# Second expert layer of the second batch element: seven block products over chunk pairs, first-layer weight parts kept in DRAM

## The chip, the cores and the metric

One NeuronCore of a Trainium2 chip runs the whole program. The metric is the device time of one execution in microseconds, as a median over runs. The engines are named as in the profile: PE (TensorE; PEld is its weight load), DVE (VectorE), ACT (ScalarE), POOL (GpSimd) and SP (SyncE, which issues the DMAs).

## The reference

Attention within clusters, then a squared-ReLU layer pair, then four experts that are weighted per token. Only the last part is touched by the change:

```python
def _moe2_ref(x, domain_probs, w1, w2):          # x is 1536 x 512: two batch elements of 768 tokens
    p = domain_probs / (domain_probs.sum(-1, keepdims=True) + 1e-09)
    out = np.zeros((N, D))
    for e in range(E):                           # E = 4 experts, F = 1024
        h = np.maximum(x @ w1[e], 0.0)           # first layer:  512 -> 1024
        out += p[:, e:e + 1] * (h @ w2[e])       # second layer: 1024 -> 512
    return out
```

All of it is float32. The kernel splits each float32 operand into a high and a low part and forms three PE products (high x high, high x low, low x high) for each product of the reference.

## The kernel before

The experts' part walks over 32 groups. A group n is one batch element (n // 16: the "first half" and the "second half" of the tokens, 768 each) and one chunk of 256 of an expert's 1024 hidden columns (16 chunks, `FQ` = 256, `NFQ` = 16).

*First layer of a group* (`product`, `block_product`, L895 to L902). Tokens (2 x 384), hidden columns (2 x 128) and the 512 inputs (2 x 256) are cut into two blocks each, and seven block products in the manner of Strassen and Winograd stand for eight. They are numbered 1, 5, 6, 2, 7, 3, 4. Each is 6 matmuls that stream 384 columns: 42 a group. Products 1, 6, 7 and 4 accumulate in one PSUM bank ("A"), 5 and 3 in another ("C"), 2 in a third ("B"). Because 6, 7 and 4 add to what is in bank A, each must wait until ACT or DVE has read the sum before it. The readings go to `fa` (`c_copy` on ACT, `c_add` on DVE), then `h_hi` (ACT: ReLU and rounding) and `h_lo` (DVE: the rest) write the parts of the hidden block into `ga` or `gb`.

*Weights of the first layer* (`fq_load`, `fq_prep`). Each group loads its 512 KB of w1 from DRAM and prepares it anew, in the second half too: the high parts on ACT, the low parts and the four sums of blocks on POOL, into the buffers `W["X"]` and `W["Y"]` (each high and low, two sides that alternate by group).

*Second layer of a group* (`token_tile`, `tile_products`, L1056 to L1097). It is a plain product: for each of the 6 tiles of 128 tokens, 6 matmuls that stream 512 columns, then one DVE instruction that multiplies by the expert's weight and adds to the output (`x2_t`). Its w2 rows are split by `second_hi` (ACT) and `second_lo` (POOL).

*Order.* It is written by hand: `group(n)` first finishes products 4 and 3 of group n - 1, runs products 1, 5, 6, 2, 7 of its own, and then the six token tiles of group n - 1, with the preparation of group n + 1 placed between them. Every engine takes its instructions in this program order. SP issues all DMAs in order; the DMAs carry eight semaphores in turn, so that one waits for the landing of the eighth before it.

Of the kernel before, what the change touches and what calls it, by code (L numbers as in the profile page):

```python
# [8 lines left out]
F32 = mybir.dt.float32  # L9
# [3 lines left out]
ALU = mybir.AluOpType  # L13
# [21 lines left out]
def moe_attention_kernel(  # L35
# [178 lines left out]
    with tc.manual_schedule():  # L214
# [755 lines left out]
        def r_lo(b, i, eng):  # L970
            eng.tensor_tensor(
                r_op(i, 1, b), t_src(b, i), r_op(i, 0, b).bitcast(F32), op=ALU.subtract)

        def fq_load(n, part=2):

            if n >= 2 * NFQ:
# [14 lines left out]

        def fq_prep(n):

            if n >= 2 * NFQ:
# [656 lines left out]

        def group(n):
            prep = fq_prep(n + 1)
            m = n - (NFQ - 6)
            if n > 1:
                fourth(n - 1)
            product(n, 1)
            c_copy(n, 0)
            if n > 1:
                third(n - 1)  # L1660
            last_relu(n - 1)
            if n == 1:
# [34 lines left out]
        NN = 2 * NFQ  # L1697
        for n in range(NN):
# [3 lines left out]
            if n:  # L1702
                group(n)
            else:
                first_group()
        fourth(NN - 1)
        third(NN - 1)
        last_relu(NN - 1)
        for t in range(NTT - 1):
            token_tile(NN - 1, t)  # L1710
        last_tile()
        mctx.close()


# [28 lines left out]
```

## Time and profile before

| | us |
|---|---|
| three timed runs: median (lowest, highest) | 1007.45 (1006.6, 1008.22) |
| the profiled execution's own time | 1007.97 |
| its span, first to last instruction | 1006.0 |
| PE busy | 998.3 |
| DVE, ACT, POOL busy | 734.4, 560.2, 607.8 |

The experts' part begins near 494 us and runs to the end. "Busy" sums the instructions of an engine; matmuls overlap, so the pace of PE is read from the chain of waits, where each piece stands with the time that it adds, and not from the mean duration of a matmul. The granted TensorE clock is 0.999 of full speed (2.4 GHz) over the whole span.

### The profile page before, as it was taken

Reading aid. Unit: us, or ns where it says so; the run is one execution under the profiler, and the core shown is the slowest. Engines: PE = TensorE matmul, PEld = TensorE weight load, DVE = VectorE, ACT = ScalarE, POOL = GpSimd, SP = SyncE. Lnnn points to the kernel's source line nnn. Section 1 sums busy time; section 2 is a strip of 40 time slices with the busy share of each in tenths; the row PEclk is TensorE's granted clock in tenths of the full one; section 3 lists DMA queues with packets and bytes.
Section 4 is the critical chain, followed back from the end, with each engine's and each line's share of the span. In section 5 each row is a group of like instructions: output and inputs, shape, how many; then the busy total and the mean of one; then the engine's idle time right before and its main releaser. Section 6 shows DMA issues by size and latency. Waiting matters only on the chain.

```text
span 1006.0 us, 15008 instructions
## 1 busy us (share of the span) xinstructions
PE 998.3 (99%) x5469; PEld 893.7 (89%) x5469; DVE 734.4 (73%) x1126; ACT 560.2 (56%) x1131; POOL 607.8 (60%) x618
## 2 busy tenths in 40 slices
PE   8999999999999999999999999999999999999998
PEld 8999999999888888888889989899899898998997
DVE  6898999888899997898585555567676555555555
ACT  6888888888655654446554344344453443444431
POOL 6468777763326604347576766767678567676671
PEclk9999999999999999999999999999999999999999
DMA  7577876862112122212012212122123221221201
GB/s 186 128 157 178 205 172 165 178 140 72 42 43 84 45 82 84 85 42 83 22 43 85 61 65 84 42 85 65 62 84 119 71 84 43 84 67 60 84 22 63
DMA packets 74082, 89.65 MB, mean 89 GB/s; under 512 B 27332, under 2 KB 50264, under 8 KB 74008
## 3 DMA queue, kind: packets, MB, share of 16 engines
q1 hardware_dynamic: 74008, 88.69, 31.9%
q8 instruction: 43, 0.70, 0.3%
q14 instruction: 31, 0.25, 0.1%
HBM read 62.58 MB, written 3.19 MB: 65 GB/s over the span
## 4 chain that ended last, share of the span: by engine, by line
PE 95%; DVE 2%; POOL 1%; DMA 1%; ACT 1%; issue 0%; SPq 0%; POOLq 0%; ACTq 0%
PE bank L900 29%; PE bank L1062 26%; PE bank L931 13%; PE s L656 6%; PE t L689 6%; PE bank L878 5%; PE po L703 3%; PE po L705 3%; PE s L878 1%; PE m L478 1%; PE m L393 1%; PE po L1114 0%; DMA k<-nkh 0%; PE m L494 0%; DVE ptl L695 0%
## 5 line engine op out<-in xcount | busy, mean ns | idle before, releaser
L1093 DVE SCALAR_TENSOR_TENSOR x<-bank,pe_p,x 128x512 f32<-128x512 f32 x179 | 134.3, 751 | 67.4 <-PE bank L1062 67.2
L1006 POOL TENSOR_TENSOR wxl<-raw,wxh 128x512 fp32r<-128x512 f32 x64 | 82.5, 1310 | 139.7 <-ACT wxh L1005 139.7
L207 ACT CAST wyh<-raw 128x512 fp32r<-128x512 f32 x64 | 39.6, 621 | 152.0 <-POOL raw L200 120.4
L1062 PE MATMUL bank<-wzh,ga 128*128 128x512 f32 (+1 forms) x392 | 121.9, 386 | 0.0
L1062 PE MATMUL bank<-wzh,gb 128*128 128x512 f32 x384 | 121.2, 390 | 0.0
L1037 DVE TENSOR_TENSOR fa<-bank,fa 128x384 f32<-128x384 f32 x96 | 53.3, 556 | 85.5 <-PE bank L900 56.4
L695 DVE TENSOR_TENSOR ptl<-t,pth 128x384 fp32r<-128x384 f32 x192 | 98.1, 549 | 20.0 <-ACT pth L694 19.6
L900 PE MATMUL bank<-xa,wxh 128*128 128x384 f32 (+1 forms) x392 | 103.9, 346 | 0.0
L665 DVE TENSOR_REDUCE nb<-s 128x1 f32<-128x768 f32 x96 | 90.9, 948 | 8.4 <-PE s L656 8.0
L694 ACT CAST pth<-t 128x384 fp32r<-128x384 f32 x192 | 83.9, 486 | 9.3 <-PE t L689 8.4
L900 PE MATMUL bank<-xa,wyh 128*128 128x384 f32 (+1 forms) x344 | 88.6, 338 | 0.0
L676 ACT ACTIVATE p<-s,nb 128x768 f32<-128x768 f32 x96 | 88.0, 916 | 0.3 <-DVE nb L665 0.2
L656 PE MATMUL s<-k,q 80*128 80x384 f32 (+1 forms) x384 | 86.5, 346 | 0.2
L1062 PEld LDWEIGHTS bank<-wzh,ga 128*128 128x128 f32 x392 | 73.3, 188 | 14.5
L689 PE MATMUL t<-identf,p 128*128 128x128 f32 x576 | 85.4, 276 | 0.4 <-DVE ptl L695 0.3
L1062 PEld LDWEIGHTS bank<-wzh,gb 128*128 128x128 f32 x384 | 72.1, 188 | 14.7
L208 POOL TENSOR_TENSOR wyl<-raw,wyh 128x512 fp32r<-128x512 f32 x64 | 84.6, 1342 | 0.0
L1034 ACT COPY fa<-bank 128x384 f32<-128x384 f32 x96 | 46.1, 480 | 66.1 <-PE bank L900 66.0
L703 PE MATMUL po<-pth,vv 128*128 128x256 f32 x288 | 80.4, 309 | 0.0
L931 PE MATMUL bank<-gb,wzh 128*128 128x512 f32 x240 | 78.0, 391 | 0.2
L900 PEld LDWEIGHTS bank<-xa,wxh 128*128 128x128 f32 x392 | 72.2, 188 | 5.6
L689 PEld LDWEIGHTS t<-identf,p 128*128 128x128 f32 x576 | 67.6, 140 | 9.5 <-DVE ptl L695 6.8
(290 smaller groups left out, 2640.8 us busy)
## 6 DMA issues: line engine op xcount, KB each, us to landing
raw<-in_moe_w_dram SPq DMA_DIRECT2D x64, 512.0 KB, 3.6
raw<-in_moe_w_in_dram SPq DMA_DIRECT2D x7, 1024.0 KB, 5.2
raw<-in_moe_w_out_dram SPq DMA_DIRECT2D x6, 1024.0 KB
k<-nkh SPq DMA_DIRECT2D x28, 192.0 KB, 3.3
q<-nqh SPq DMA_DIRECT2D x28, 192.0 KB, 4.1
nv<-in_v_dram SPq DMA_DIRECT2D x16, 192.0 KB, 4.1
out_dram<-x SPq DMA_DIRECT2D x11, 256.0 KB, 2.0
k<-nkl SPq DMA_DIRECT2D x14, 192.0 KB, 3.4
```

The costliest lines, as they stand in the source:

```text
L208: return lambda: eng.tensor_tensor(lo, a[m], hi.bitcast(F32), op=ALU.subtract)
L656: nc.tensor.matmul(s[:, j, 0:HALF], stk[i, nq][:, t * 128:(t + 1) * 128], stk[i, nk][:, j * HALF:(j + 1) * HALF], start=first, stop=not first)
L665: nc.vector.tensor_reduce(out=nb, in_=s_ps[u][:, :, 0:HALF], axis=AX.XY, op=ALU.max, negate=True)
L676: nc.scalar.activation(p, s_ps.pop(u)[:, :, 0:HALF], AF.Exp, bias=nb_t.pop(u), accum_out=sums_t[hp][:, i % 2, t:t + 1])
L689: nc.tensor.transpose(tp[:, j], p_sb[u][:, half, j * 128:(j + 1) * 128], identf)
L694: return (lambda: nc.scalar.copy(dh, tp), lambda: nc.vector.tensor_tensor(dl, tp, dh.bitcast(F32), op=ALU.subtract))
L695: lambda: nc.vector.tensor_tensor(dl, tp, dh.bitcast(F32), op=ALU.subtract))
L703: nc.tensor.matmul(po_t[pr], vt[i][:, kt], pth[:, kt], start=(kt == 0), stop=False)
L900: nc.tensor.matmul(ps, w[:, ks], x(xx)[:, kt], start=(first and kt == 0 and z == 0), stop=(kt == 1 and z == 2), skip_group_check=True)
L931: nc.tensor.matmul(o, a[:, d], b, start=(ft == 0 and z == 0), stop=(ft == 1 and z == 2))
L1062: nc.tensor.matmul(o, a, w[:, f, cols], start=(f == 0 and z == 0), stop=(f == 1 and z == 2))
L1093: nc.vector.scalar_tensor_tensor(out=acc, in0=o, scalar=pc, in1=acc, op0=ALU.mult, op1=ALU.add)
```

## The change

The first half of the tokens keeps its groups. What is new:

- *Kept weights.* At the end of each group n of the first half `keep(n + 1)` writes the prepared parts of the next chunk (six DMAs, 1.8 MB) to a DRAM tile. In the second half `back(n)` reads them into the same buffers; the loads and the preparation of chunks 18 to 31 are gone (16 and 17 are prepared as before).
- *Second layer of the second half.* Two chunks of one expert make a pair m (8 pairs). Their hidden blocks (tokens 2 x 384, hidden 2 x 256) and w2 (hidden 2 x 256, outputs 2 x 256) are again multiplied by seven block products (`second_product`). Each is 3 token tiles x 6 matmuls that stream 256 columns: 126 matmuls a pair, where six tiles of two groups had 72 that stream 512. After each tile one DVE instruction of 128 x 256 adds it to the output: 21 a pair, where 12 of 128 x 512 stood.
- *Operands.* The steps S, H, L (hidden blocks of 128 x 768: sums on DVE, high parts on ACT, low parts on DVE) and t, y, z (w2 blocks of 128 x 512: sums on POOL, high parts on ACT, low parts on POOL) make the operands of the seven products. R is a ReLU on ACT. Each operand has one buffer.
- *Order.* The two layers are interleaved by a written sequence. A pass over pair m runs its seven second-layer products (m1, m5, m6, m2, m7, m3, m4), with first-layer products of later chunks between them, and the steps of the next pair hang on these events. Before the first pass, chunks 16 to 19 run their first layer with nothing but the last token tiles of the first half between (the *hand-over*); the last pass but one has only two first-layer products left, the last has none.

```diff
+        ORDER2 = (1, 5, 6, 2, 7, 3, 4)
+        kept = {n: mp["hb"].tile([128, 4096], F32, name=f"kept{n}") for n in range(2, NFQ)}
+        KEPT = [("X", 0, 2), ("Y", 0, 4), ("X", 3, 4)]
+        def keep(n):
...
+                    nc.sync.dma_start(
+                        out=kept[n][:, o + a * 256:o + b * 256],
+                        in_=W[t][x][:, p + a * 256:p + b * 256].bitcast(F32))
...
+        def h_sum(m, i, eng=nc.vector):
+            if i == 5:
+                nc.vector.scalar_tensor_tensor(
+                    out=hx(m, 1, 0), in0=hx(m, 1, 1), scalar=0.0, in1=hx(m, 1, 0), op0=ALU.max, op1=ALU.add)
...
+            elif i == 7:
+                eng.tensor_tensor(hsum(m), hx(m, 0, 0), hx(m, 1, 0), op=ALU.subtract)
...
+        def first_product(n, i):
+            m, q = divmod(n - NFQ, 2)
+            product(n, i)
...
+            if i == 1:
+                nc.scalar.copy(hx(m, 0, q)[:, 0], a)
+            elif i == 5:
+                nc.scalar.copy(hx(m, 1, q)[:, 1], c)
+            elif i == 6:
+                nc.scalar.copy(hx(m, 1, q)[:, 0], a)
+            elif i == 4:
+                nc.scalar.activation(hx(m, 0, q)[:, 1], a, AF.Relu)
+                if n != NFQ + 1:
+                    back(n + 2)
+            else:
...
+                nc.vector.tensor_tensor(o, z, o, op=ALU.add)
...
+        def second_product(m, i):
...
+            for j in range(3):
+                o = {"A": bank[5 + j][:, 0:256], "C": bank[(2, 3, 1)[j]][:, 0:256],
+                     "B": bank[(4, 0, 4)[j]][:, 256 * (j == 2):][:, 0:256]}[b]
...
+                    for z, (a, w) in enumerate(((hh, wh), (hh, wl), (hl, wh))):
+                        nc.tensor.matmul(
+                            o, a, w, start=(i in (1, 5, 2) and f == 0 and z == 0),
+                            stop=(f == 1 and z == 2), skip_group_check=True)
...
+                    nc.vector.scalar_tensor_tensor(
+                        out=acc, in0=o, scalar=pc, in1=acc, op0=ALU.mult, op1=ALU.add)
...
+        SECOND = {"m1": "H1 y1 z1 t5 t7", "4b": "S5", "m5": "L1 H5", "m6": "S6 y5 z5 t6",
+                  "m2": "H2 H6 y6 y2 z6 z2 t4", "m7": "H7", "m3": "y7 y3 z7 z3", "m4": "H4 y4 z4"}
+        NEXT = {"5a": "L5", "6a": "L6", "7a": "L2", "1b": "S3", "3a": "H3 L7", "4a": "N1",
+                "5b": "L3", "6b": "L4"}
+        SAME = {"7a": "R0", "6b": "R1", "2b": "S7g"}
+        LATE = dict(SECOND, m2=SECOND["m2"] + " L5", m3=SECOND["m3"] + " L6", m4="H4 y4 z4 L7g")
+        LAST = {"m1": "L2 S3", "m5": "H3 L3g", "m6": "L4"}
+        FIRST = {(17, 1): "y5 z5 t6", (17, 5): "R1", (17, 2): "y6 y2 z6 z2 t4 S7g", (17, 4): "S5 H1 L1",
+                 (18, 5): "H5 S6", (18, 6): "L5 y7 y3 H6 z7 z3", (18, 2): "L6", (18, 7): "H2 y4 z4 L2",
...
+        first_product(NFQ, 5)
+        for f in prep[0:2]:
+            f()
+        for i in (6, 2, 7):
+            first_product(NFQ, i)
+        for t in range(NTT):
+            token_tile(NFQ - 1, t)
+            if t == 0:
+                steps(0, "R0")
+                first_product(NFQ, 3)
+                first_product(NFQ, 4)
...
+        for m in range(NM):
...
+            seq = "m1 3p 4p m5 m6 m2 m7 m3 1a m4 5a 6a 2a 7a 1b 3a 4a 5b 6b 2b 7b".split()
```

In `seq`, a and b are the two chunks of the pair after next, and p is the second chunk of the next pair (its products 3 and 4 come a pass later).

*ACT at the hand-over.* Before, between products 1 and 6 of a group of the second half (the two COPY rows), ACT had one ReLU of the group before:

```order
L1043 ACTIVATE ga<-bank_4442 128x384 [waits PE_49]
L1034 COPY fa<-bank_4441 128x384 [waits PE_49,Activation_49]
L1043 ACTIVATE ga<-fa 128x384 [waits DVE_49]
L1034 COPY fa<-bank_4441 128x384 [waits PE_49,Activation_49]
L1015 CAST wzh<-raw 128x1024 [waits DMAHW5_49]
```

Now, around product 5 (L1818) and product 6 (L1820) of chunk 18, it has the operand steps H1 and H5 (L1800), the copies, y7 and y3 (L1767) and H6:

```order
L1822 ACTIVATE fa<-bank_4444 128x384 [waits PE_49,Activation_49]
L1800 CAST xa<-fa 128x768 [waits Activation_49]
L1818 COPY x_4452<-bank_4445 128x384 [waits DMAHW0_49,DMAHW3_49,DVE_49,PE_49]
L1800 CAST xa<-fa 128x768 [waits DVE_49]
L1820 COPY x_4452<-bank_4443 128x384 [waits PE_49]
L1767 CAST ga<-raw 128x512
L1767 CAST wzh<-raw 128x512
```

The copy of product 6 out of bank A (4443) now stands behind H5, which waits for the DVE's S5.

*POOL and DVE at the hand-over.* Before, POOL went from one chunk's preparation to the next; now, behind the last preparation (L208), it makes z1, t5 and t7, z5, t6, z6, z2, t4 and S7 (L1792):

```order
L208 TENSOR_TENSOR wyl<-raw,wyh 128x512 [waits PE_49,Activation_49]
L1770 TENSOR_TENSOR wzl<-raw,wzh 128x512 [waits DMAHW7_49,Activation_49]
L1764 TENSOR_TENSOR raw<-raw 128x2x256 [waits Pool_49] x2
L1770 TENSOR_TENSOR wzl<-raw,wzh 128x512 [waits Activation_49]
L1764 TENSOR_TENSOR raw<-raw 128x512
L1770 TENSOR_TENSOR gb<-raw,gb 128x512 [waits DVE_49,Activation_49]
L1770 TENSOR_TENSOR gb<-raw,gb 128x512 [waits Activation_49]
L1764 TENSOR_TENSOR raw<-raw 128x2x256 [waits Pool_49]
L1792 TENSOR_TENSOR raw<-fa 128x768 [waits DVE_49]
```

The DVE's row S5 (L1785), first of the steps that follow the additions of chunk 17, waits for POOL:

```order
L1827 TENSOR_TENSOR fa<-bank_4446,fa 128x384 [waits PE_49,Activation_49]
L1785 SCALAR_TENSOR_TENSOR fa<-fa 128x2x384 [waits DVE_49,Pool_49]
L1808 TENSOR_TENSOR xa<-fa,xa 128x768 [waits Activation_49]
L1794 TENSOR_TENSOR fa<-fa 128x768 [waits DVE_49]
L1808 TENSOR_TENSOR xa<-fa,xa 128x768 [waits Activation_49]
L1827 TENSOR_TENSOR x_4451<-bank_4447,x_4451 128x384 [waits DMAHW0_49,PE_49]
```

S5 overwrites a block that S7 reads, so the whole row of POOL steps now stands ahead of it.

*DVE near the end.* Before, in the last groups, the six token tiles came with two short `h_lo` between them:

```order
L1093 SCALAR_TENSOR_TENSOR x_4449<-bank_4446,pe_p,x_4449 128x512 [waits PE_49]
L1046 SCALAR_TENSOR_TENSOR ga<-fa,ga 128x384 [waits Activation_49]
L1093 SCALAR_TENSOR_TENSOR x_4449<-bank_4447,pe_p,x_4449 128x512 [waits PE_49]
L1046 SCALAR_TENSOR_TENSOR ga<-fa,ga 128x384 [waits Activation_49]
L1093 SCALAR_TENSOR_TENSOR x_4450<-bank_4448,pe_p,x_4450 128x512 [waits PE_49]
L1093 SCALAR_TENSOR_TENSOR x_4450<-bank_4446,pe_p,x_4450 128x512 [waits PE_49]
```

Now, in the last pass but one, L5 and L6 (L1808) stand around the readings of m7 and m3, ahead of those of m4 (banks 4448 to 4450) and of the next pass's m1 (the last row):

```order
L1808 TENSOR_TENSOR xa<-x_4452,xa 128x768 [waits Activation_49]
L1861 SCALAR_TENSOR_TENSOR x_4452<-bank_4448,pe_p,x_4452 128x256 [waits PE_49]
L1861 SCALAR_TENSOR_TENSOR x_4451<-bank_4449,pe_p,x_4451 128x256 [waits PE_49]
L1861 SCALAR_TENSOR_TENSOR x_4452<-bank_4450,pe_p,x_4452 128x256 [waits PE_49]
L1861 SCALAR_TENSOR_TENSOR x_4451<-bank_4445,pe_p,x_4451 128x256 [waits DVE_49,PE_49]
L1861 SCALAR_TENSOR_TENSOR x_4451<-bank_4446,pe_p,x_4451 128x256 [waits DVE_49,PE_49]
L1861 SCALAR_TENSOR_TENSOR x_4452<-bank_4444,pe_p,x_4452 128x256 [waits DVE_49,PE_49]
L1808 TENSOR_TENSOR xa<-x_4451,xa 128x768 [waits Activation_49]
L1861 SCALAR_TENSOR_TENSOR x_4452<-bank_4448,pe_p,x_4452 128x256 [waits PE_49]
L1861 SCALAR_TENSOR_TENSOR x_4451<-bank_4449,pe_p,x_4451 128x256 [waits PE_49]
L1861 SCALAR_TENSOR_TENSOR x_4452<-bank_4450,pe_p,x_4452 128x256 [waits PE_49]
L1861 SCALAR_TENSOR_TENSOR x_4451<-bank_4448,pe_p,x_4451 128x256 [waits DVE_49,PE_49]
```

The m4 of one pass and the m1 of the next use the same three banks, and here no first-layer product stands between them.

## Rows read from the trace of the kernel before

**Rows 1.** The page, part 1: busy us, share of span, instructions.

```profile
PE 998.3 (99%) x5469; PEld 893.7 (89%) x5469; DVE 734.4 (73%) x1126; ACT 560.2 (56%) x1131; POOL 607.8 (60%) x618
```

**Rows 2.** The page, part 4: the chain that ended last, by engine.

```profile
PE 95%; DVE 2%; POOL 1%; DMA 1%; ACT 1%; issue 0%; SPq 0%; POOLq 0%; ACTq 0%
```

**Rows 3.** Busy time of each engine in the second half's stretch.

```profile
core 0: us, PE busy (x) PEld busy (x) DVE busy (x) ACT busy (x) POOL busy (x), PEclk, DMA share, GB/s
766.00:991.00 225.00, 225.00 (x1129) 203.50 (x1129) 125.94 (x191) 91.37 (x172) 147.65 (x127) 1.00 0.19 61
```

**Rows 4.** The chain in order of time: start us, us added, line, count.

```profile
735.66 8.20 PE bank L1062 x36
743.86 7.30 PE bank L900 x42
...
994.07 8.86 PE bank L1062 x48
```

**Rows 5.** The same chain in the attention: matmuls of 128 x 256.

```profile
100.13 0.12 PE po L703
...
100.72 0.12 PE po L705
100.84 0.70 PE s L656 x4
```

**Rows 6.** Groups by line and shape, DVE: count | busy us, mean ns | idle before.

```profile
L1093 DVE SCALAR_TENSOR_TENSOR x<-bank,pe_p,x 128x512 f32<-128x512 f32 x179 | 134.3, 751 | 67.4 <-PE bank L1062 67.2
L1037 DVE TENSOR_TENSOR fa<-bank,fa 128x384 f32<-128x384 f32 x93 | 51.7, 557 | 85.3 <-PE bank L900 56.4 <-ACT fa L1034 28.8
L1046 DVE SCALAR_TENSOR_TENSOR gb<-fa,gb 128x384 fp32r<-128x384 f32 x45 | 35.0, 778 | 8.9 <-ACT gb L1043 8.9
L1046 DVE SCALAR_TENSOR_TENSOR ga<-bank,ga 128x384 fp32r<-128x384 f32 x16 | 8.9, 556 | 12.6 <-ACT ga L1043 12.6
L971 DVE TENSOR_TENSOR rt<-x,rt 128x768 fp32r<-128x768 f32 x3 | 2.8, 945 | 0.0
L1074 DVE SCALAR_TENSOR_TENSOR x<-bank,pe_p,x 128x256 f32<-128x256 f32 x1 | 0.5, 483 | 0.0
```

**Rows 7.** Groups by line and shape, ACT.

```profile
L1034 ACT COPY fa<-bank 128x384 f32<-128x384 f32 x91 | 43.7, 480 | 63.6 <-PE bank L900 63.6
L207 ACT CAST wyh<-raw 128x512 fp32r<-128x512 f32 x60 | 37.3, 621 | 150.1 <-POOL raw L200 119.7 <-POOL raw L202 30.4
L968 ACT CAST xa<-x 128x768 fp32r<-128x768 f32 x3 | 2.5, 825 | 0.0
```

**Rows 8.** Groups by line and shape, POOL.

```profile
L208 POOL TENSOR_TENSOR wyl<-raw,wyh 128x512 fp32r<-128x512 f32 x60 | 79.2, 1340 | 0.0
```

**Rows 9.** Timeline of POOL, then DVE, where the second half begins: start, us.

```profile
749.31 2.17 POOL L971 TENSOR_TENSOR xa<-x,xa 128x768 fp32r<-128x768 f32 x1
754.39 2.30 POOL L1006 TENSOR_TENSOR wxl<-raw,wxh 128x512 fp32r<-128x512 f32 x2 [2.90 <-ACT wxh L1005]
759.92 2.54 POOL L208 TENSOR_TENSOR wyl<-raw,wyh 128x512 fp32r<-128x512 f32 x2
...
749.70 2.61 DVE L971 TENSOR_TENSOR xa<-x,xa 128x768 fp32r<-128x768 f32 x1
752.23 1.01 DVE L1037 TENSOR_TENSOR fa<-bank,fa 128x384 f32<-128x384 f32 x2
```

**Rows 10.** Timeline of ACT there.

```profile
748.07 0.82 ACT L968 CAST xa<-x 128x768 fp32r<-128x768 f32 x1
749.18 0.48 ACT L1034 COPY fa<-bank 128x384 f32<-128x384 f32 x1 [0.29 <-PE bank L900]
753.70 0.91 ACT L1005 CAST wxh<-raw 128x512 fp32r<-128x512 f32 x2
```

**Rows 11.** DMA, 518 to 990 us: packets, MB, share of 16 engines; issues, landing us.

```profile
q1 hardware_dynamic: 24144, 32.06, 21.1%
...
raw<-in_moe_w_dram SPq DMA_DIRECT2D x57, 512.0 KB, 3.6
```

**Rows 12.** The chain's last piece.

```profile
1002.96 0.35 DVE x L1074
```

More of the change, by code (lines that the diff above doesn't have):

```diff
@@ L974, in fq_load @@
         def fq_load(n, part=2):
-            if n >= 2 * NFQ:
+            if n >= NFQ + (2 if part == 0 else 0):
                 return
@@ L1691, in group @@
                     r_lo(1, RB11, nc.vector)
+            keep(n + 1)
             fq_load(n + 3, 0)
@@ L1695, in group @@
                 t_sum(1, (RT3, RT1, RT2, None, RT4)[m])
-        NN = 2 * NFQ
-        for n in range(NN):
+        ORDER2 = (1, 5, 6, 2, 7, 3, 4)
+        kept = {n: mp["hb"].tile([128, 4096], F32, name=f"kept{n}") for n in range(2, NFQ)}
+        KEPT = [("X", 0, 2), ("Y", 0, 4), ("X", 3, 4)]
+        def keep(n):
+            if n not in kept:
+                return
+            p = (n % 2) * 1024
+            for t, a, b in KEPT:
+                for x in range(2):
+                    o = 2048 * (t == "Y") + x * 1024
+                    nc.sync.dma_start(
+                        out=kept[n][:, o + a * 256:o + b * 256],
+                        in_=W[t][x][:, p + a * 256:p + b * 256].bitcast(F32))
@@ new lines, in back @@
+        def back(n, parts=KEPT):
+            if n >= 2 * NFQ:
+                return
+            p = (n % 2) * 1024
+            for t, a, b in parts:
+                for x in range(2):
+                    o = 2048 * (t == "Y") + x * 1024
+                    nc.sync.dma_start(
+                        out=W[t][x][:, p + a * 256:p + b * 256].bitcast(F32),
+                        in_=kept[n - NFQ][:, o + a * 256:o + b * 256])
+        W_AT = {1: ("X", 0, 1), 5: ("Y", 3, 4), 6: ("Y", 0, 1), 2: ("X", 1, 2),
+                7: ("Y", 2, 3), 3: ("Y", 1, 2), 4: ("X", 3, 4)}
@@ new lines, in h_hi2, with h_lo2 @@
+        def h_hi2(m, i):
+            if i in (2, 4):
+                nc.scalar.activation(h_op(i, 0), h_val(m, i), AF.Relu)
+            else:
+                nc.scalar.copy(h_op(i, 0), h_val(m, i))
+        def h_lo2(m, i, eng=nc.vector):
+            hi = h_op(i, 0).bitcast(F32)
+            if i in (2, 4):
+                nc.vector.scalar_tensor_tensor(
+                    out=h_op(i, 1), in0=h_val(m, i), scalar=0.0, in1=hi, op0=ALU.max, op1=ALU.subtract)
+            else:
+                eng.tensor_tensor(h_op(i, 1), h_val(m, i), hi, op=ALU.subtract)
@@ new lines, in acc_half @@
+        def acc_half(t, d):
+            if t < 4:
+                return x2_t[t // 2][:, t % 2, S + 256 * d:S + 256 * d + 256]
+            return x2_t[t - 4][:, d, S + 512:2 * S]
+        BLOCK = {1: (0, 0), 5: (1, 1), 6: (0, 1), 2: (0, 0), 7: (1, 1), 3: (0, 1), 4: (1, 0)}
+        def second_product(m, i):
+            e = m // (NQ // 2)
+            last = m == NFQ // 2 - 1
+            r, d = BLOCK[i]
+            b = PROD[i][2]
+            for j in range(3):
+                o = {"A": bank[5 + j][:, 0:256], "C": bank[(2, 3, 1)[j]][:, 0:256],
+                     "B": bank[(4, 0, 4)[j]][:, 256 * (j == 2):][:, 0:256]}[b]
+                js = slice(j * 128, (j + 1) * 128)
+                for f in range(2):
+                    hh, hl = [h_op(i, z)[:, f, js] for z in range(2)]
+                    wh, wl = [y_op(i, z)[:, f] for z in range(2)]
+                    for z, (a, w) in enumerate(((hh, wh), (hh, wl), (hl, wh))):
+                        nc.tensor.matmul(
+                            o, a, w, start=(i in (1, 5, 2) and f == 0 and z == 0),
+                            stop=(f == 1 and z == 2), skip_group_check=True)
+                t = 3 * r + j
+                pc = pe_p[:, NTT + t, e:e + 1]
+                acc = acc_half(t, d)
+                if m == 0 and i in (1, 5, 6, 4):
+                    nc.vector.tensor_scalar(acc, o, pc, None, op0=ALU.mult)
+                else:
+                    nc.vector.scalar_tensor_tensor(
+                        out=acc, in0=o, scalar=pc, in1=acc, op0=ALU.mult, op1=ALU.add)
+                if last and i in (2, 7, 3, 4):
+                    nc.sync.dma_start(out=ov[1, t][:, 256 * d:256 * d + 256], in_=acc)
@@ new lines, in call, with steps @@
+        def call(f, *a):
+            return lambda: f(*a)
+        FS = {"H": h_hi2, "L": h_lo2, "S": h_sum, "R": h_relu, "y": y_hi, "z": y_lo, "t": y_sum,
+              "N": lambda m, i: load_second(m + i)}
+        def steps(m, ws):
+            for w in ws.split():
+                FS[w[0]](m, int(w[1]), *([nc.gpsimd] if w[2:] else []))
+        NM = NFQ // 2
+        SECOND = {"m1": "H1 y1 z1 t5 t7", "4b": "S5", "m5": "L1 H5", "m6": "S6 y5 z5 t6",
+                  "m2": "H2 H6 y6 y2 z6 z2 t4", "m7": "H7", "m3": "y7 y3 z7 z3", "m4": "H4 y4 z4"}
@@ L1699, in moe_attention_kernel @@
+        for n in range(2 * NFQ):
             pb[n, "A"] = bank[n % 2]
@@ L1701, in moe_attention_kernel @@
             pb[n, "B"] = bank[4] if n else bank[3]
[L1702 to L1711, printed above, removed]
+        first_group()
+        for n in range(1, NFQ):
+            group(n)
+        load_second(0)
+        fourth(NFQ - 1)
+        prep = fq_prep(NFQ + 1)
+        first_product(NFQ, 1)
@@ new lines, in moe_attention_kernel @@
+        third(NFQ - 1)
+        last_relu(NFQ - 1)
+        first_product(NFQ, 5)
[9 more added lines that the diff above has]
+                first_product(NFQ, 4)
+            elif t == 1:
+                prep[2]()
+            elif t == 3:
+                steps(0, "y1 z1 t5 t7")
@@ new lines, in moe_attention_kernel @@
+        for n, i in [(1, 1), (1, 5), (1, 6), (1, 2), (1, 7), (2, 1), (1, 3), (1, 4), (2, 5), (2, 6), (2, 2),
+                     (2, 7), (3, 1), (2, 3), (2, 4), (3, 5), (3, 6), (3, 2), (3, 7)]:
+            first_product(NFQ + n, i)
+            steps(0, FIRST.get((16 + n, i), ""))
+            ev = "%d%s" % (i, " ab"[n - 1])
+            if n > 1:
+                steps(1, SAME.get(ev, ""))
+        for m in range(NM):
+            a, b = NFQ + 2 * m + 4, NFQ + 2 * m + 5
+            seq = "m1 3p 4p m5 m6 m2 m7 m3 1a m4 5a 6a 2a 7a 1b 3a 4a 5b 6b 2b 7b".split()
+            if m + 2 >= NM:
+                seq = [x for x in seq if x[1] not in "ab" and (x[1] != "p" or m + 2 == NM)]
+            for ev in seq:
+                if ev[0] == "m":
+                    second_product(m, int(ev[1]))
+                else:
+                    first_product({"p": a - 1, "a": a, "b": b}[ev[1]], int(ev[0]))
+                ev = ev.replace("p", "b") if ev in ("3p", "4p") else ev + "_" if ev in ("3b", "4b") else ev
+                if m + 2 < NM:
+                    steps(m + 1, SECOND.get(ev, ""))
+                    steps(m + 1, NEXT.get(ev, ""))
+                    steps(m + 2, SAME.get(ev, ""))
+                elif m + 2 == NM:
+                    steps(m + 1, LATE.get(ev, ""))
+                else:
+                    steps(m, LAST.get(ev, ""))
```

79 lines of the change are left out of this document (64 added, 15 removed).

## The prediction

> **What bounds the kernel now.** I read the page's busy times first, then the chain of waits, then the second half's stretch, then groups by shape. PE is busy for 998.3 of 1006.0 us [rows 1], and the chain that ended last is 95% PE [rows 2]: the time is PE's, and the other engines count only where PE waits for them. In the experts' second half PE is busy in all 225.00 us of the stretch, at full clock (1.00), while DVE has 125.94, ACT 91.37 and POOL 147.65, so DVE and POOL are at 56 and 66% [rows 3]. The chain shows PE's own pace: a group's first layer is 42 matmuls of 384 columns in 7.30 us, 0.1739 us each; its second layer is 36 of 512 columns in 8.20 us, 0.2278 us each [rows 4]. A pair of groups takes 31.0 us.
>
> The two paces differ by 0.0539 us for 128 columns, and 0.0539 x 4 = 0.2156 leaves 0.012 us of a 512-column matmul that doesn't shrink with its width. For 256 columns that line gives 0.1200 us. The attention has such matmuls, each with its own weight load: six from 100.13 to 100.84 us, 0.118 each [rows 5]. I take 0.120; 0.118 would be 2 us better over the half.
>
> **PE's work.** The first layer is the same 42 matmuls a group. The second layer before: 16 groups x 8.20 us = 131.2, and 0.7 more because the last piece, split finer, took 8.86 [rows 4]: 131.9. After: 8 pairs x 126 x 0.120 = 121.0. **Minus 10.9 us**, not the eighth of 131 (16.4) that seven products for eight suggest: 126 narrow matmuls carry the fixed part more often than 72 wide ones.
>
> *A rule beside this.* The Trainium skill ("TensorE: Matmul & The Clock Gate", section "Wait — 56ns, not 53.3ns?") gives a gap of columns / 2.4 plus 2.5 ns for one matmul. By it 72 wide ones take 15.5 us and 126 narrow ones 13.8, an estimated 14.2 us less over the half. The trace disagrees with it: 0.2278 against 0.2158 us at 512 columns. That the small fixed part holds for the new matmuls all the same is a rival below.
>
> **The other engines in a steady pass.** PE needs 84 x 0.1739 + 126 x 0.120 = 29.7 us.
> DVE: 21 readings of 0.483, 6 additions of 0.557 and 10 steps on 128 x 768 of 0.945 [rows 6] are 23.0 us; back to back an instruction holds the engine some 0.1 us less than its mean (two additions together took 1.01 [rows 9]), so about 20.
> ACT: 8 readings of 0.480, 7 casts of 0.621 and 9 or so wide ones of 0.825 or less [rows 7], about 15.5.
> POOL: 11 of 1.340 [rows 8] and one of 128 x 768, nearer 1.9: 16.6, while 8 subtractions and 4 sums a group for the weights are gone.
> All fit in 29.7, if DVE and POOL don't block each other. They do: at 749.70 a 128 x 768 subtraction of DVE took 2.61 us beside POOL's at 749.31 (2.17) [rows 9], where such steps alone take 0.945; and L1046 takes 0.778 us on two SBUF operands against 0.556 with one in PSUM [rows 6]. With a mean wait of 0.2 us a step (that difference), DVE has 22 to 25 us. Walking a pass with these durations, the nearest deadlines hold by 0.3 to 0.8 us: m7's accumulation after m6's readings, 4a after the DVE's addition of 7a, 7a after ACT's copy of 6a, 7b after the copy of 6b, which queues behind H3 and so behind DVE's S3. I take 0.8 us for the six full passes together, between 0 and 3 (0.5 each).
>
> The Trainium skill ("SBUF — State Buffer", section "Who interferes with whom") says that DVE, with two SBUF inputs, and GpSimd take a shared port pair by an exclusive lock. The 2.61 us agree.
>
> **Hand-over: four waits.** Here first-layer products of chunks 16 to 19 run with six token tiles only as cover.
> (a) The copy of product 6 of chunk 16 now queues on ACT behind the cast that began at 748.07, the copy of 5 (0.48) and the two weight casts (0.91, at 753.70 before) [rows 10]; it ends near 750.5. Product 7 would start at 749.97: **0.55 us**.
> (b) POOL's preparation of chunk 17 starts when POOL's and DVE's swap of the token blocks are done, at 752.3, and lasts what it lasted from 754.39 to 762.46 [rows 9]: 760.4. Then come z1, t5, t7, z5, t6, z6, z2, t4 (1.25 to 1.34 each) and S7 (1.9): 772.5. S5 waits for S7, H5 for S5, and the copy of (18, 6) stands behind H5 on ACT: 772.5 + 0.95 + 0.83 + 0.48 + hops = 775.1. Without waits PE would reach product (18, 7), which needs that copy, at 772.8. So (a) and (b) together are 2.3 us, set by POOL.
> (c) (18, 4) needs DVE's addition of (18, 7), which stands behind L1, S6, L5 and L6, and L6 behind H6, y3 and y7 on ACT: 0.5 us, 1.1 if z7 blocks a step.
> (d) (19, 7) needs the copy of (19, 6), behind H3 and H4 on ACT, behind S3 on DVE, which z3 and z4 can block: 0.4 to 2.4.
> Sum 3.2 to 5.8; with a late POOL up to 6.5. **I take 4.2**, nearer the lower end, since the durations in the walk are means and hold the engines a little too long.
>
> **End.** In the last pass but one DVE must also do L5 and L6 before the readings of m4, and m1 of the last pass overwrites m4's banks at once. With no blocking DVE keeps up (0); with each of five steps blocked by up to one POOL instruction of 1.34 the first reading of m4 comes 3.3 us after PE wants the bank. I take 1.2. The last reading is 0.483 instead of 0.35 us [rows 6, 12]: 0.1.
>
> **DMA.** `keep` adds 1.8 MB of writes to a group of 15.5 us, `back` 3.7 MB of reads to a pass, less 1 MB of w1. In the second stretch the engines moved 32.06 MB in 21.1% of 472 us, 322 GB/s when busy [rows 11]. First half: 2.9 MB in 15.5 us is 187 GB/s, 58%; second: 4.7 MB in 29.7 us, 160 GB/s, half. On SP's queue the loads stand behind the six `keep` DMAs, 6 us more; they are used over 10 us later. `back` is issued after a chunk's product 4, 12 us or more before the next use. Cover: those 12 us. I cost it at 0; a landing that is late would add up to 6 us once, at the hand-over.
>
> **Sum,** on the profiled execution's own 1007.97 us (1006.0 of span): - 10.9 + 4.2 + 0.8 + 1.2 + 0.1 = - 4.6, so 1003.4. The median of the three runs, 1007.45, lies 0.5 below that execution, so 1002.9 for the median; **forecast 1003 us**. Its own range, with the ends of each term (3.3 to 12.9 us of waits): 999.4 to 1009.
>
> **Rivals.**
> *The steady pass becomes DVE's (slower).* DVE's ten wide steps meet POOL's instructions in every pass. DVE has 20 us plus ten waits of w; it passes 29.7 at w = 0.96. For: w was 1.67 in the one case where both queues were full [rows 9]. Against: 0.2 on average over 45 instructions with POOL 66% busy [rows 3, 6], and POOL has 56% of a pass now, mostly not where DVE has most steps. At w = 1.2 a pass takes 32.1, 2.4 more, six times 14.4: 1017 us. It is slower than before from w = 1.04.
> *The cover holds.* The waits of the hand-over and the end don't reach PE, because POOL and ACT run ahead of my walk: 1007.45 - 10.9 + 0.1 = 996.7 us. Against: S5's wait for POOL stands in the program's order, and POOL's row of steps is long.
> *The fixed part vanishes at 256 columns.* The new matmuls would cost seven eighths of the old, 131.9 - 115.4 = 16.5 us less, with the same waits: 997 us. Against: the six matmuls of 128 x 256 [rows 5]. The skill's rule above points this way.
> *Late weights.* Kept parts or w2 blocks land after PE wants them, about 1 us a pass or 6 at the hand-over: 1009 us. Against: half of the DMA engines' time is free.
>
> **How the numbers follow.** About 0.2% (2 us) is what a measurement of this kernel can tell from no change: faster means below 1005.4, slower above 1009.5. Forecast 0.63, of which three quarters lie below 1005.4 (0.47) and the rest within (0.16), since both waits at their ends give up to 1009. DVE-bound passes 0.17: 0.15 slower, 0.02 within. Cover holds 0.12 and smaller fixed part 0.03: faster. Late weights 0.05: 0.02 within, 0.03 slower. That makes faster 0.62, same 0.20, slower 0.18. The range: 997.5 leaves out half of the cases of full cover, 1011 most of the DVE-bound ones, together under 0.2.
>
> **What would show it.** In the profile after: the chain's pieces of the new matmul line, 18 in 2.16 us (2.2 and more would say that the fixed part is larger); PE without idle time in the passes and about 30 us from m1 to m1; gaps of PE before (16, 7), (18, 7), (18, 4) and (19, 7), the second the largest and ended by ACT; on DVE S5 waiting for POOL; near the end m1 waiting for DVE's reading of m4. If PE is busy without gaps and DVE too is under 80%, the cover held. If wide DVE steps average over 1.9 us and every pass has gaps before m7 or 4a, the passes are DVE's. If PE waits for a DMA, the weights were late. I would be wrong at the root if 256-column matmuls in this stream took 0.125 us or more: 1,008 of them at that pace use up the 4.6 us.

## The result: slower by 8.4 us, and the profile after

The changed kernel takes 1016.1 us (median of 4 runs, 1014.7 to 1017.5), the kernel before 1007.7 beside it. The ratio is 1.0085, 95% interval 1.0068 to 1.0103: slower, and above the range of the prediction. The profiled execution has a span of 1014.3 us, 8.3 more than before.

Page of the changed kernel, part 1 (busy us, share of the span, instructions) and part 4 (the chain that ended last):

```profile
PE 991.1 (98%) x5889; PEld 906.0 (89%) x5889; DVE 787.6 (78%) x1209; ACT 576.2 (57%) x1139; POOL 609.6 (60%) x589
...
PE 83%; DVE 7%; POOL 4%; DMA 2%; issue 2%; ACT 1%; SPq 0%; DVEq 0%; POOLq 0%; ACTq 0%
```

PE was busy for 7.2 us less [rows 1], and its share of the chain fell from 95% [rows 2] to 83%: PE has less to do and now waits. DVE's part of the chain rose from 2% to 7%. The waits of PE in the second half, by line and by what ended them (us in total, times, longest us):

```profile
PE bank L1852 <- DVE x L1861: 10.3, 8, 2.5
PE bank L900 <- ACT x L1820: 3.4, 2, 2.0
PE bank L900 <- DVE x L1827: 0.5, 1, 0.5
PE bank L900 <- ACT fa L1820: 0.4, 1, 0.4
PE bank L1852 <- ACT fa L1822: 0.3, 1, 0.3
```

The first row is what the prediction doesn't have. Eight waits, one in each pass: the second layer's matmuls (L1852) wait for a DVE reading of the second layer (L1861). The other rows are the hand-over, and one of two short waits for ACT.

The view leaves out the hops between engines, so I also measured every stall as the time that PE falls behind its own pace (0.1739 us for a first-layer matmul, 0.120 for a second-layer one) in the rows of the timeline. Before, there is none over 0.25 us from 494 us on. After:

| where (start of the delayed matmul, us) | stall, us |
|---|---|
| hand-over: 749.56, 774.69, 778.62, 784.43 | 0.56 + 2.20 + 0.69 + 1.51 = 4.96 |
| last tile of m2, six full passes | 1.69 + 1.18 + 1.19 + 0.95 + 1.03 + 1.18 = 7.22 |
| last tile of m2, last two passes | 1.67 + 2.68 = 4.35 |
| before m5, two passes | 0.40 + 0.48 = 0.88 |
| last tile of m2 and m7 of the last pass, at a lower clock | 1.59 |
| sum | 19.0 |

With the forecast 10.9 us less work, 19.0 - 10.9 = + 8.1, against 8.3 of span (with the 10.6 that experiment 5 shows below, + 8.4). The account closes.

**The wait that was not foreseen.** First PE, then DVE, in the pass around 857 us (start us, us, operation, tiles, count, and in brackets the idle time before with what ended it):

```profile
854.96 3.76 PE L1852 MATMUL bank<-gb,xa 128*128 128x256 f32 x30
859.75 0.98 PE L1852 MATMUL bank<-gb,xa 128*128 128x256 f32 x6 [1.03 <-DVE x L1861]
...
855.23 0.48 DVE L1861 SCALAR_TENSOR_TENSOR x<-bank,pe_p,x 128x256 f32<-128x256 f32 x1 [0.52 <-PE bank L1852]
855.63 1.63 DVE L1808 TENSOR_TENSOR xa<-x,xa 128x768 fp32r<-128x768 f32 x1
857.18 1.26 DVE L1861 SCALAR_TENSOR_TENSOR x<-bank,pe_p,x 128x256 f32<-128x256 f32 x3
858.36 0.94 DVE L1794 TENSOR_TENSOR x<-x,x 128x768 f32<-128x768 f32 x1
859.22 0.86 DVE L1861 SCALAR_TENSOR_TENSOR x<-bank,pe_p,x 128x256 f32<-128x256 f32 x2
```

The 30 matmuls are m6 (18) and two tiles of m2 (12); the last 6 of m2 come 1.19 us late. `second_product` gives product 2's three tiles the banks 4, 0 and 4: the first tile lies in the lower half of bank 4, the third in its upper half. The program lets the third tile's first matmul wait until the first tile has been read. In the order of the changed program, that wait stands in the middle of m2 on PE:

```
L1852 MATMUL bank_4447<-gb,xa 128x256
L1852 MATMUL bank_4447<-gb,xa 128x256 [waits Pool_49]
...
L1852 MATMUL bank_4443<-gb,xa 128x256 x6
L1852 MATMUL bank_4447<-gb,xa 128x256 [waits DVE_49]
```

PE needs 0.72 us for the tile between. On DVE the awaited reading (the first of the two at 859.22) stands behind L1 (855.63), the three readings of m6 and S6 (858.36). So PE gets ahead of DVE and is stopped there, by 1.19 us in this pass and by 0.95 to 1.69 in the six full ones. The 1.69 of the first pass and the 1.67 of the last but one come where S6 took 2.08 and 2.06 us; in the five passes between it took 0.94.

### The profile page after: what moved, and what is told of

It reads as the page before. It is cut to its first block, busy times and chain, and to the rows that moved or that the text cites. A ratio compares the mean times of both kernels' runs of the same rounds, so it can differ in the third digit from the quotient of the medians.

```text
span 1014.3 us, 16370 instructions
## 1 busy us (share of the span) xinstructions
PE 991.1 (98%) x5889; PEld 906.0 (89%) x5889; DVE 787.6 (78%) x1209; ACT 576.2 (57%) x1139; POOL 609.6 (60%) x589
## 4 chain that ended last, share of the span: by engine, by line
PE 83%; DVE 7%; POOL 4%; DMA 2%; issue 2%; ACT 1%; SPq 0%; DVEq 0%; POOLq 0%; ACTq 0%
PE bank L900 23%; PE bank L931 12%; PE bank L1062 11%; PE bank L1852 8%; PE s L656 6%; PE t L689 6%; PE bank L878 5%; PE po L703 3%; PE po L705 3%; DVE x L1861 2%; DMA raw<-in_moe_w_dram 2%; DVE xa L1808 1%; PE s L878 1%; PE m L478 1%; PE m L393 1%
## 5 line engine op out<-in xcount | busy, mean ns | idle before, releaser
L1861 DVE SCALAR_TENSOR_TENSOR x<-bank,pe_p,x 128x256 f32<-128x256 f32 x156 | 72.8, 480 | 35.2 <-PE bank L1852 34.4
L1078 DVE SCALAR_TENSOR_TENSOR x<-bank,pe_p,x 128x512 f32<-128x512 f32 x90 | 67.6, 751 | 35.8 <-PE bank L1062 35.7
L1006 POOL TENSOR_TENSOR wxl<-raw,wxh 128x512 fp32r<-128x512 f32 (+1 forms) x36 | 47.1, 1328 | 70.1 <-ACT wxh L1005 70.1
L900 PE MATMUL bank<-rt,wyh 128*128 128x384 f32 (+1 forms) x264 | 71.4, 351 | 3.8 <-ACT x L1820 3.4
L705 PE MATMUL po<-ptl,vv 128*128 128x256 f32 x288 | 72.5, 281 | 0.0
L900 PE MATMUL bank<-xa,wxl 128*128 128x384 f32 (+1 forms) x196 | 67.7, 345 | 0.0
L207 ACT CAST wyh<-raw 128x512 fp32r<-128x512 f32 x36 | 22.3, 622 | 78.1 <-POOL raw L200 60.7
L1770 POOL TENSOR_TENSOR wzl<-raw,wzh 128x512 fp32r<-128x512 f32 x32 | 49.9, 1562 | 26.9 <-ACT wzh L1767 26.9
L656 PEld LDWEIGHTS s<-k,q 80*128 80x128 f32 (+1 forms) x384 | 63.4, 189 | 0.6 <-ACT p L676 0.2
L900 PEld LDWEIGHTS bank<-xa,wyh 128*128 128x128 f32 x344 | 62.0, 188 | 1.4
```

The costliest lines, as they stand in the source:

```text
L656: nc.tensor.matmul(s[:, j, 0:HALF], stk[i, nq][:, t * 128:(t + 1) * 128], stk[i, nk][:, j * HALF:(j + 1) * HALF], start=first, stop=not first)
L705: nc.tensor.matmul(po_t[pr], vt[i][:, kt], ptl[:, kt], start=False, stop=(kt == NTT - 1))
L900: nc.tensor.matmul(ps, w[:, ks], x(xx)[:, kt], start=(first and kt == 0 and z == 0), stop=(kt == 1 and z == 2), skip_group_check=True)
L1861: nc.vector.scalar_tensor_tensor(out=acc, in0=o, scalar=pc, in1=acc, op0=ALU.mult, op1=ALU.add)
```

## Experiments

**1. Product 2: multiply all three tiles, then read them.** No tile is then written into a bank that a reading of the same product still holds.

```
+            todo = [("p", 0), ("p", 1), ("p", 2), ("r", 0), ("r", 1), ("r", 2)]
+            if i != 2:
+                todo = [(w, j) for j in range(3) for w in "pr"]
-            for j in range(3):
+            for what, j in todo:
...
```

"p" stands for a tile's six matmuls, "r" for its reading.

> The changed kernel, but in product 2 of the second layer all three tiles' matmuls are issued before the first reading, so no tile of it is written into a bank that a DVE reading of the same product still holds. Theory, shared bank: the last tile of m2 waits in each of the eight passes (1.0 to 2.7 us, 11.6 us together) only because it lies in the upper half of bank 4, whose lower half DVE reads behind a long row of other steps. Then these eight gaps go, nothing else moves, and the time falls from 1016.1 to 1004 to 1006 us, a little faster than the kernel before. Rival, passes bound by DVE: DVE is late because it has too much to do; then the gaps come back before m7, m4 or product 4 of the first layer, 0.5 to 1.7 us a pass, and the time stays at 1011 or more. A mix is possible in the last pass alone (2.7 us of the 11.6), where DVE has two more wide steps.

Measured: 1002.9 us, ratio to the kernel before 0.995 (0.9936 to 0.9963), 13.3 us under the changed kernel and 1.1 under the expected 1004 to 1006. PE's waits in the second half:

```profile
PE bank L900 <- ACT x L1820: 2.6, 2, 2.0
PE bank L1855 <- ACT fa L1822: 0.4, 1, 0.4
PE bank L900 <- ACT fa L1820: 0.4, 1, 0.4
PE bank L1855 <- ACT x L1822: 0.4, 1, 0.4
```

No wait for a second-layer reading is left, none has come before m7 or m4, and all stalls together fell from 19.0 to 5.7 us: the 13.3 that the time fell. Of these, 11.6 are the eight waits; 1.6 the lower clock after the longest of them, which the expected time had not counted. DVE ran as many steps as before (1209 on both pages), so the eight waits came from the shared bank, not from too much work on DVE.

**2. S6 behind the readings of m2, banks left shared.**

```
...
-        "m6": "S6 y5 z5 t6",   "m2": "H2 H6 y6 y2 z6 z2 t4"
+        "m6": "y5 z5 t6",      "m2": "S6 H2 H6 y6 y2 z6 z2 t4"
```

> The changed kernel with DVE's step S6 (one 128 x 768 subtraction, 0.95 us alone, up to 1.9 beside POOL) queued behind the readings of m2 instead of ahead of them; the banks stay shared. Theory, shared bank behind a long row on DVE: the wait of m2's last tile is as long as what stands ahead of the reading, so it shrinks by the length of S6: in the six passes with S6 there from 1.0 to 1.7 us each to 0 to 0.7, 6 to 7 us together, and the time is about 1009 to 1010 us; the last two passes keep their waits. Rival, DVE-bound passes: the work of DVE is the same, so the waits only move to m7 or m4, and the time is 1014 to 1016 us.

Measured: 1008.5 us, ratio 1.0009 (1.0 to 1.0018), half a microsecond under the expected 1009 to 1010. DVE in the same pass:

```profile
855.02 2.07 DVE L1861 SCALAR_TENSOR_TENSOR x<-bank,pe_p,x 128x256 f32<-128x256 f32 x5
857.74 0.48 DVE L1861 SCALAR_TENSOR_TENSOR x<-bank,pe_p,x 128x256 f32<-128x256 f32 x1 [0.65 <-PE bank L1852]
858.14 1.43 DVE L1794 TENSOR_TENSOR x<-x,x 128x768 f32<-128x768 f32 x1
```

The reading of m2's first tile is now the fourth of the five at 855.02, ahead of S6. PE's stall in that pass is 0.32 us instead of 1.19; in the six full passes none is over that. The last pass keeps its 2.7, as expected; the last but one loses its 1.67 too, which I had not expected, although its S6 comes from the same table and was moved too. So the wait is as long as the row of DVE steps ahead of the reading.

**3. The next pass's second-layer weights loaded earlier.**

```
-        "7a": "L2", ... "4a": "N1"
+        "7a": "L2 N1"
```

> The changed kernel with the load of the next pass's second-layer weights issued after product 7 of the even chunk, ahead of the twelve transfers that bring kept parts back, instead of behind them. Theory, late weights: the two gaps before m5 (0.40 and 0.48 us) come from this load landing after ACT wants it, which holds the ReLU of product 4 back on ACT; they vanish, and the time is 1015.2 us, 0.9 less, hardly to be told from the changed kernel by its time, but to be seen as gaps in the trace. Rival, ACT's own row is too long: the gaps stay as they are. If the kept parts now land too late instead, new waits of PE on a transfer show in the first layer.

Measured: 1017.6 us (1016.5 to 1017.7), ratio 1.0095. What it was to remove is seen in the changed kernel's ACT, where the cast of the new weights waits for their transfer and the ReLU of product 4 (L1822) stands behind it; then in the same place the cast with the early load, which waits for nothing:

```profile
821.92 0.62 ACT L1767 CAST wzh<-raw 128x512 fp32r<-128x512 f32 x1 [1.78 <-DMA raw<-in_moe_w_dram]
822.45 0.49 ACT L1822 ACTIVATE fa<-bank 128x384 f32<-128x384 f32 x1
```

```profile
819.72 0.61 ACT L1767 CAST wzh<-raw 128x512 fp32r<-128x512 f32 x1
```

Both stalls before m5 are gone, as the theory had it. Yet the kernel is no faster: m2's stall is now 1.69 us in five of the six full passes (0.61 in the first). The reason is S6 (L1794). First the changed kernel, then this run, three of the passes from 800 to 980 us (min/median/max ns, first and last start), each with POOL's subtraction z5 (L1770) in the pass around 858 us; for this run S6 of that pass stands between them:

```profile
L1794 DVE TENSOR_TENSOR fa<-fa x3: 941/943/943, 827.2 to 951.4; 128x768 f32<-128x768 f32 x3
...
858.37 2.06 POOL L1770 TENSOR_TENSOR wzl<-raw,wzh 128x512 fp32r<-128x512 f32 x1
```

```profile
L1794 DVE TENSOR_TENSOR fa<-fa x3: 2073/2073/2076, 825.8 to 951.6; 128x768 f32<-128x768 f32 x3
...
857.29 2.08 DVE L1794 TENSOR_TENSOR x<-x,x 128x768 f32<-128x768 f32 x1
...
857.26 1.28 POOL L1770 TENSOR_TENSOR wzl<-raw,wzh 128x512 fp32r<-128x512 f32 x1
```

POOL works beside S6 in both kernels. In the changed kernel S6 begins 0.01 us ahead of z5 (858.36 and 858.37); S6 then takes 0.94 us and z5 2.06. With the weights in time POOL's row comes earlier and z5 begins 0.03 us ahead (857.26 and 857.29); z5 takes 1.28 us and S6 2.08. L1, which stands ahead of S6, takes 0.95 there for 1.63. The net is half a microsecond more ahead of the same reading. While the bank is shared, freeing ACT only moves the collision.

**4. Another order of side steps at the hand-over.**

```
...
-        first_product(NFQ, 5);  prep[0](); prep[1]();  first_product(NFQ, 6)
+        first_product(NFQ, 5);  first_product(NFQ, 6);  prep[0](); prep[1]()
-  (17, 5): "R1", (17, 2): "y6 y2 z6 z2 t4 S7g", (18, 2): "L6", (18, 7): "H2 y4 z4 L2",
-  (18, 4): "H3 H4 N1", (19, 5): "L3", (19, 6): "L4"
+  (17, 5): "R1 S7g", (17, 2): "y6 y2 z6 z2 t4", (18, 7): "L6 H2 y4 z4 L2",
+  (18, 4): "N1", (19, 6): "H3 H4", (19, 7): "L3 L4"
```

> The changed kernel with another order of the side steps at the hand-over alone: the copy of product 6 of chunk 16 ahead of the two weight casts on ACT; POOL's difference S7 of the first pass three weight steps earlier; the casts H3 and H4 behind the copy of product 6 of chunk 19; L3, L4 and L6 behind the additions they stood ahead of. Theory, order of the queues: PE's four gaps there (0.56, 2.20, 0.69 and 1.51 us, together 4.96) are each a reading that stands behind one of these steps, and fall to 0 to 1.5 us together; the time is 1011 to 1013 us. Rival, too little cover: POOL's and ACT's work at the hand-over is more than six token tiles hide, so the gaps turn up at later products or before m1 and m5 (3 to 5 us together), and the time stays at 1015 to 1016 us.

Measured: 1012.9 us, ratio 1.0056 (1.0043 to 1.0069). Waits of PE in the second half:

```profile
PE bank L1852 <- DVE x L1861: 9.3, 8, 2.5
PE bank L900 <- DVE x L1827: 2.2, 1, 2.2
PE bank L1852 <- DVE x L1827: 0.8, 1, 0.8
PE bank L1852 <- ACT x L1822: 0.6, 1, 0.6
```

All three waits for ACT's copies (0.56, 2.20 and 1.51 us) are gone: they were a matter of order. But the wait for DVE's addition of (18, 7) grew from 0.69 to 2.37, and a new one of 0.94 came before m5, so 3.3 us of the 5.0 are left (and about 1 us at a lower clock after the longer one). The chain says why (start us, us added):

```profile
768.82 1.94 DVE fa L1785
770.75 1.98 DVE xa L1808
...
774.63 2.04 DVE xa L1808
776.66 0.94 DVE x L1827 x2
```

S5, L1, S6 and L5 stand ahead of the addition, and beside a busy POOL each takes about 2 us instead of 0.95. The expected time of 1011 to 1013 us was met; the expected 0 to 1.5 us of stalls was not.

**5. Experiments 1 and 3 together, and a second order at the hand-over.** Ahead of the addition of (18, 7) only S5 and L1 stay on DVE; L6 and L3 go to POOL, L4 behind m2.

```
...
+  (17, 5): "R1 S7g", (17, 2): "y6 y2 z6 z2 t4", (17, 4): "S5 H1 L1", (18, 5): "H5",
+  (18, 6): "y7 y3 z7 z3", (18, 7): "S6 L5 H2 y4 z4", (19, 1): "H6 L6g H7 L7g",
+  (18, 4): "L2 S3 N1", (19, 6): "H3 L3g", (19, 7): "H4"      first pass, m2: "L4"
```

> The changed kernel with three edits together: product 2's three tiles multiplied ahead of their readings; the next pass's weights loaded after product 7; and a second order for the hand-over: copy of product 6 of chunk 16 ahead of the two casts, S7 earlier on POOL, S6, L5, L2, S3, H3, H4 behind the addition of (18, 7) or later, L6 and L3 on POOL, L4 after m2. Left in the run with product 2 alone were 5.7 us of gaps: 4.6 at the hand-over, with about 1.1 us in which PE ran at a lower clock after its longest gap, and 1.1 before m5. Theory, order of the queues: they fall to 0 to 2 us, and with them the time from 1002.9 to 997 to 999.5 us. Rival, too little cover at the hand-over: DVE and POOL have too much to do there, 2 us or more of waiting turn up before m5 to m7 of the first pass, and the time is 1000 to 1002 us.

Measured: 997.3 us, ratio to the kernel before 0.9899 (0.9885 to 0.9912): faster than both kernels. All waits of PE in the second half, and a pass of its chain:

```profile
PE bank L1855 <- ACT x L1822: 0.3, 1, 0.3
```

```profile
841.51 2.15 PE bank L1855 x18
...
845.74 10.79 PE bank L1855 x90
...
871.17 2.15 PE bank L1855 x18
```

From m1 (841.51) to m1 (871.17) a pass takes 29.66 us, and all pieces of the chain between them are PE's own work. The span, 995.9 us, is 10.1 under that of the kernel before, with 0.46 us of stalls left. S6 takes 2.07 us in this kernel too, in all passes but the first, and PE no longer waits behind it.

**6. No writes to DRAM and none back.** `keep` and `back` issue nothing, so that products of the second half use whatever weights lie in the buffers.

```
         def keep(n):
-            if n not in kept:
+            if True:
                 return
         def back(n, parts=KEPT):
-            if n >= 2 * NFQ:
+            if True:
                 return
```

> The changed kernel without the writes of weight parts to DRAM and without the reads that bring them back: that part of the computation is left out, and products of the second half use whatever weights lie there; all else stays. Theory, the traffic costs nothing but the late load of the next weights, which now comes early: the gaps before m5 (0.4 and 0.5 us) go, the eight waits of product 2 and the four of the hand-over stay, and the time is 1014 to 1016.5 us. Rival, the traffic slows DVE, POOL or PE's operands, or its transfers hold PE: 1010 us or less, with shorter steps on DVE and POOL.

Measured: 1018.5 us (1018.0 to 1018.6), ratio 1.011, 2 us more than the changed kernel. From 790 us on the DMA engines are busy for 10% here and 37% in the changed kernel, and PE still waits at the hand-over and in every m2, so the traffic does not hold it. As in experiment 3 the weights come in time, the stalls before m5 go, S6 takes 2.06 to 2.08 us every time and m2's stall is 1.67 to 1.69 in each full pass. The upper end of the expected time was missed by 2 us: I had left the waits of m2 as they were, and they grew.

**7. Experiment 1 with one wide DVE step more in seven passes.**

```
-        "m5": "L1 H5"
+        "m5": "L1 L1 H5"
```

> The run with product 2's tiles multiplied ahead of their readings, and DVE's step L1 (128 x 768) done twice, once more than needed, in the six full passes and the last but one. It asks how much room DVE has left in a pass. Theory, shared bank (DVE has spare time once no reading holds the bank): 81% busy leaves some 6 us a pass, an extra step of 0.95 to 2 us is hidden, and the time is 1002.5 to 1004.5 us. Rival, passes near the DVE's bound: 1 to 2 us more in each pass, 1009 to 1016 us.

Measured: 1005.6 us (1004.9 to 1006.1), ratio 0.9982 (0.9973 to 0.9991), 2.7 more than experiment 1. The larger of the two groups of L1808 into xa, first in experiment 1, then here (count | busy us, mean ns):

```profile
L1808 DVE TENSOR_TENSOR xa<-x,xa 128x768 fp32r<-128x768 f32 x12 | 17.6, 1488 | 0.0
```

```profile
L1808 DVE TENSOR_TENSOR xa<-x,xa 128x768 fp32r<-128x768 f32 x16 | 24.2, 1528 | 0.1
```

The other group, from fa, went from 9 steps and 14.4 us to 12 and 20.1 (both groups from 780 us on). DVE has 12.3 us more to do (44.3 for 32.0), and 2.7 of them reach the end: it has room, though not all of the 6 us a pass that I expected, since five of the passes now stall before m7 (three by 0.38 us, two by 0.16), where a reading of m6 comes too late, and the last pass by 0.55 before m1. The time lies a microsecond above the expected range and far below the rival's.

## Why the prediction was wrong

**The step that failed: the list of deadlines in a steady pass.** It compared products with each other (m7 behind m6's readings, 4a behind the addition of 7a, ...), and found 0.3 to 0.8 us of room. The deadline within a product, m2's third tile behind the reading of its first, was not on the list, although the shared bank is in the diff and the wait in the order of the program. By the prediction's own durations (a step 0.1 us under its mean, a wide one 0.2 longer) it fails. From 855.23, where the trace has m5's last reading, DVE needs 0.39 for a reading, 1.05 for L1, 1.18 for three readings, 1.05 for S6 and 0.39, in all 4.06, which gives 859.3; PE wants the bank at 854.96 + 30 x 0.120 = 858.56. That is 0.7 us a pass, without any long step. The term of 0.8 us for all six passes measured 7.2, and 0.9 more for the late weights.

The Trainium skill ("PSUM — Partial Sum Buffer", section "PSUM bank collisions raise a hardware error") has the rule that would have put it on the list: two engines must not touch the same bank in the same partitions at once, even at different columns. By it the two halves of bank 4 are one resource, and while the third tile lies there the wait itself can't be dropped, only what makes it long. The trace agrees as far as it goes: PE waits for a reading of the other half. What happens without the wait no run here shows; it wasn't tried.

**The end: the place was wrong and the size too small.** I had m1 of the last pass wait for m4's readings (1.2 us, 0 to 3.3). It does not wait in this kernel; it does by 0.47 and 0.55 us in experiments 2 and 7. Instead m2 waits. The 1.67 us of the last but one pass are the steady pass's wait with a long S6 (1.98 us in the chain, from 981.75). The 2.68 of the last pass come from the wide steps that this pass adds on DVE. The chain's end:

```profile
994.32 1.05 DVE xa L1805
...
995.39 1.93 DVE x L1788
...
999.68 1.95 DVE gb L1805
1001.62 0.41 DVE x L1861
...
1002.07 8.96 PE bank L1852 x60
```

L2, S3 and L4 (994.32, 995.39, 999.68) stand ahead of the awaited reading, 0.41 us at 1001.62. The 60 matmuls then took 8.96 us for 7.2; 1.59 of the difference is the lower clock (below), a term that the sum did not have.

**PE's work: right.** 18 of the new matmuls take 2.15 us, 0.1195 each, for the 0.120 worked out from [rows 4]. Experiment 5, which has next to no waits, is 10.1 us of span under the kernel before; with its 0.46 us of stalls that is 10.6 us less work, for the 10.9 that were forecast. The rival that the fixed part vanishes (16.5) falls.

**Hand-over: right in mechanism and size.** 4.96 us for 4.2 (3.2 to 6.5). Product 7 of chunk 16 waits 0.56 (forecast 0.55). The chain of the second wait is the one that was walked, and ends 0.5 us from it:

```profile
770.60 1.81 POOL raw L1792
...
772.44 0.97 DVE fa L1785
...
773.43 0.83 ACT xa L1800
774.26 0.38 ACT x L1820
```

S7 on POOL ends at 772.4 (forecast 772.5), S5 and H5 follow, the copy of (18, 6) ends at 774.6 (775.1). (18, 4) waits 0.69 (0.5 to 1.1), (19, 7) 1.51 (0.4 to 2.4). Experiment 4 took three of the four away by order alone.

**The rivals.** *Passes bound by DVE* gave 1017 us, near the result, and is wrong all the same: experiment 1 has the same DVE steps and no wait for second-layer readings, and experiment 7 hides most of an extra step. What it had right is the price of a collision: L1808 into xa averages 1.52 us over the 21 steps from 780 us on in the changed kernel (31.9 us), 0.57 above the 0.945 of [rows 6], where I took 0.2 for all wide steps. That the times agree is chance. *Late weights* happens, in two passes with 0.40 and 0.48 us; without it the time was no better. *The cover holds* falls for the kernel as changed.

**DMA at nothing: right** but for that load. The kept parts themselves were never what PE waited for (its waits above name no transfer), and without their traffic the kernel was no faster (experiment 6).

**The range of the sum.** Its ends were taken 0.5 us too low: 1007.45 - 10.9 with 3.3 and 12.9 us of waits gives 999.9 and 1009.5. The result lies above either.

## What to carry to other kernels

When a product is split into more tiles than it has banks, write down who must have read what before each tile's first matmul, inside a product as well as between products, and count what stands ahead of that reading on its engine. An engine with a fifth of its time to spare can still stop PE in every pass; what decides is the row of steps between a result and its reading. Issue a product's matmuls first and its readings behind them where two tiles share a bank, before anything is done about the engine's load.

## What the runs showed of the hardware

**After its longest waits PE often ran at the lower clock, though not always.** The last pass of the changed kernel, in slices of 1 us (busy us of PE and instructions, granted clock, DMA share, GB/s):

```profile
1001.00:1002.00 1.00, 0.00 (x0) 1.00 0.00 0
1002.00:1003.00 1.00, 0.93 (x6) 0.79 0.09 31
1003.00:1004.00 1.00, 1.00 (x7) 0.50 0.70 232
...
1006.00:1007.00 1.00, 1.00 (x10) 1.00 0.39 131
```

PE had been idle for 2.5 us; after that some 3 us run at 0.50, the 1.2 GHz level, and m7 takes 3.41 us for 2.15. Of the twelve waits of 2.0 to 2.6 us in this kernel and experiments 1 to 7, eight were followed by such a stretch (some 1.0 to 1.6 us lost) and four were not, among them the same wait of 2.04 us before (18, 7): clock 1.00 after it in the changed kernel, 0.50 in experiment 1. Behind the waits of 1.7 us or less no lower clock was seen. The clock also differs between runs of one kernel: of the eleven of experiment 2 three had a mean clock of 1.000 over the span (1007.1 to 1007.6 us), the others 0.998 or less (1008.3 to 1009.8). What decides it stays open. The prediction priced a wait at its length alone.

Such a stretch need not reach the end of the kernel. In experiment 1 the one at the hand-over cost 1.1 us, but PE then reached (18, 4) without a wait and waited 0.72 us for 1.51 before (19, 7): 4.6 us for the hand-over in all, 5.0 in the changed kernel without it.

**A wide DVE step has two prices, and a start 0.01 us earlier can decide which.** S6 took 0.94 us in every steady pass from 800 to 980 us of the changed kernel and 2.07 in every such pass of experiments 3 and 5. In all 35 passes with an S6 of the changed kernel and of experiments 1, 3, 5 and 6, POOL's z5 begins within 0.04 us of it. Where S6 was first, it took 0.94 us and z5 2.05 to 2.09; where z5 was first, it took 1.28 or 1.29 and S6 2.06 to 2.08. So the two ran nearly one after the other: 0.94 and 1.28 are 2.22 us, and the second of them was done 2.05 to 2.09 us after its own start. The Trainium skill ("SBUF — State Buffer", section "Who interferes with whom") says that a shared port pair, which DVE uses for a second SBUF input, is an exclusive lock between DVE and GpSimd; these prices agree. A mean between them describes none of the passes.
